# Three columns of a two-row product taken row by row in two chunks of a fused recurrence and feed-forward kernel

## The chip, the cores and the metric

The kernel runs on one core of one Trainium2 chip. A core has TensorE (PE: matrix products, with its weight loads shown apart as PEld), VectorE (DVE), ScalarE (ACT), GpSimd (POOL) and SyncE (SP), each with its own queue of instructions, taken in order. Products land in PSUM, which has eight banks of 128 partitions by 512 float32; everything else sits in SBUF. DMA transfers are issued from the queues of SP, POOL and ACT. The metric is the device time of one execution in microseconds (us), lower is better.

## The reference

A gated linear recurrence over 768 steps, for 4 batch rows and 8 heads of dimension 48, is followed by a bilinear feed-forward layer on the 3072 tokens (4 x 768) of width 8 x 48 = 384, with a hidden width of 1536. All inputs and the output are float32.

```
for t in range(S):
    state = alpha[:, :, t, :, None] * state + einsum('bhd,bhe->bhde', k[:, :, t], v[:, :, t])
    y[:, :, t] = einsum('bhd,bhde->bhe', q[:, :, t], state)
x = y.transpose(0, 2, 1, 3).reshape(B * S, H * D)
out = ((x @ w_a) * (x @ w_b)) @ w_out
```

## The kernel before

The work is cut into six chunks, 0 to 5. A chunk is two batch rows by 256 steps: chunk c takes rows `c % 2 * 2` and the one after it, and the third `c // 2` of the steps. For each chunk the kernel first does the recurrence in its chunked form, with logarithms of alpha, cumulative sums, exponentials, scores and a carried state, and then the feed-forward layer on the chunk's 512 tokens.

The order of all instructions is written out by hand, in the string `PROGRAM` (lines 17 to 258). A line is `chunk: operation; operation; ...`. The program is walked from top to bottom and every operation appends its instructions to the queues of the engines it uses, so the order in `PROGRAM` is the order on each engine; engines run ahead of one another as far as the data, the PSUM banks and the buffers allow. The operations that matter here:

- `XT u` (line 762): the DMA transpose, issued from SP, that brings row u of x from `ys` into `xT`. `X u` before it copies the finished row from PSUM to `ys`. `xT` has a part for each row u = 0, 1. In chunk 2 the program has `XT 1` first and `XT 0` after it; in chunk 3 it has `XT 0` first.
- `a f w i` and `b f w i` (line 777): the gate and the up product of column f (f = 0 to 11, 128 hidden units each) into PSUM bank i. Each is three matmuls, over three slices of the 384 model columns. `w` is `*` for both rows at once (512 tokens wide), `0` or `1` for one row (256 tokens wide, and half of the bank).
- `as f w` (line 783): ScalarE copies the gate product from PSUM to a buffer in SBUF. There are three such buffers, and a half takes a whole one.
- `pr f w` (line 791): VectorE multiplies that buffer with the up product in PSUM, into `prod`.
- `o m h i` (line 799): half h of the output product of token block m; `ot m E` evicts it on engine E (V is VectorE, S is ScalarE), `st m Y` stores it, from SP.
- `lx V` (lines 424 and 427): VectorE adds the logarithms of the even and odd steps of a later chunk, in three instructions. `R 0` and `R 1` (line 488): VectorE takes the remainders after rounding of these sums; `AQ` then uses both.
- `mk u`, `mq u` (line 543): VectorE multiplies keys and queries with their decays; `T u` (line 595), from SP, transposes the result.
- `lv` (line 517) scales keys or queries on VectorE or POOL; `E` are exponentials and `ra` a ratio on ScalarE; `ld` are loads; `dr` and `dl` write the decays to memory and load them again (lines 549 and 554); `K`/`KA`, `k` (lines 653 and 654), `D`, `M`, `Mc`, `Mm`, `SB`, `SA` and `Y` are the recurrence's own state, scores and outputs.

A PSUM bank may be written again only when its last reader is done: for a gate product that is `as`, for an up product it is `pr`, for an output it is `ot`. The bank numbers in `PROGRAM` are chosen by hand.

Chunks 0 and 1 take many of their columns one row at a time. Chunks 2 to 5 take every column with both rows at once. The feed-forward work of chunk 2 begins behind the output products of chunk 1 and is mixed with the preparations of chunks 3 and 4; that of chunk 3 begins behind the output products of chunk 2 and is mixed with those of chunks 4 and 5.

Of the kernel before, what the change touches and what calls it, by code (L numbers as in the profile page):

```python
# [138 lines left out]
1: o 0 1 -; ot 0 V; a 1 1 6; a 10 1 1; as 1 1; as 10 1  # L139
3: E 0 b; E 0 i  # L140
1: b 4 1 2; pr 4 1; b 8 1 5; b 1 1 1; a 8 1 6; b 10 1 0; pr 1 1; o 3 0 2; pr 10 1; as 8 1; pr 8 1; o 3 1 -; ot 3 S; st 3 Y
2: a 4 * 7; as 4 *
3: E 1 b
2: a 5 * 6; b 4 * 3
3: E 1 i
1: st 0 Y
3: dr; ld k * P; lv 0 k P; lv 1 k P
4: lx V; R 0
3: mk 0 V; mq 0 V; T 0
4: ld q * Y  # L150
2: a 1 * 2; b 5 * 0; as 5 *; pr 5 *
4: ra 1
2: b 7 * 4; b 10 * 1; pr 4 *; a 10 * 6; as 10 *; pr 10 *
3: mk 1 V
2: a 7 * 0; b 1 * 5; a 0 * 6; b 0 * 7; as 1 *; as 7 *; pr 1 *; pr 7 *; as 0 *; a 3 * 0; b 9 * 1; pr 0 *
3: mq 1 V; ld v * P
5: ld a * P
2: as 3 *; b 3 * 2; a 9 * 6
4: ra 0
2: pr 3 *; as 9 *; pr 9 *; a 2 * 5  # L160
4: lv 0 q P
2: as 2 *; b 2 * 7; pr 2 *
3: KA * 06; D 0 0 4; M 0 0; dl; k * 0 V; k * 1 V
# [21 lines left out]
2: o 2 0 1; o 2 1 -; o 3 0 6; o 1 0 0; o 3 1 -; o 1 1 -  # L185
4: dr
1: st 1 Y
3: a 11 * 5
2: ot 2 V; ot 3 V
4: mq 0 V; mk 0 V  # L190
5: lx V
3: a 9 * 3; a 0 * 2; a 8 * 6; b 11 * 7; as 9 *; as 11 *; as 0 *; pr 11 *; b 9 * 2; b 0 * 1; pr 9 *
5: lv 0 k V
3: as 8 *
2: ot 1 S
3: b 8 * 3; a 5 * 4; as 5 *; a 6 * 6; a 4 * 7; pr 0 *; pr 8 *
5: R 0
4: mq 1 V
3: b 5 * 3; a 1 * 1; pr 5 *; as 4 *; b 6 * 7; as 6 *; pr 6 *
4: ld v * P; K * 0 2; T 0; D 0 1 5  # L200
3: as 1 *
4: D 0 0 3; Mc 0 0; dl; k * 0 V
# [753 lines left out]
```

## Time and profile before

| what | value |
|---|---|
| median of 3 runs | 196.31 us (195.17 to 201.79) |
| the profiled execution's own time | 196.55 us |
| its span, first to last instruction | 194.8 us |
| instructions | 5851 |
| PE busy | 183.4 us (94%) |
| VectorE busy | 137.2 us (70%) |
| ScalarE busy | 103.0 us (53%) |
| POOL busy | 55.8 us (29%) |
| gate and up products, line 777 | 113.2 us of PE in 540 matmuls |
| output products, line 799 | 48.5 us of PE in 276 matmuls |
| mean granted clock of TensorE | 1.000 |

The profile is of one execution. Its times count from the start of the span. A row of a timeline gives the start, the time from the first start to the last end of the instructions that it merges, the engine, the line, the operation with output and input, the count, and in brackets how long the engine had been idle before it and what it then waited for. Matmuls overlap one another in the array, so their pace is read from start to start, not from the duration of one. The chain is the sequence of work that ended last, followed back from the last instruction.

### The profile page before, as it was taken

What the parts mean: (1) busy time and instruction counts of PE and PEld (TensorE: products, weight loads), DVE (VectorE), ACT (ScalarE), POOL (GpSimd) and SP (SyncE); (2) the same over time, 40 slices, a digit from 0 to 9 for tenths busy, and PEclk for the clock granted to TensorE, in tenths of its full rate; (3) what the DMA queues carried; (4) which work ended last, traced back from release to release, by engine and by line L of the source; (5) the groups of instructions that cost most, each with busy time, mean ns of one, the idle gap of its engine ahead of it and who ended that gap; (6) DMA issues with size and microseconds to landing.
All of it is one profiled execution on the core that took longest, in us unless ns stands there. A gap on an engine that the chain in (4) does not pass through costs nothing.

```text
span 194.8 us, 5851 instructions
## 1 busy us (share of the span) xinstructions
PE 183.4 (94%) x2498; PEld 111.5 (57%) x2498; DVE 137.2 (70%) x230; ACT 103.0 (53%) x189; POOL 55.8 (29%) x75
## 2 busy tenths in 40 slices
PE   1998899899999999999998989999999999999993
PEld 1577675566687877644555534555544556544463
DVE  3588966999899796779979379786755871147520
ACT  4465766686765668555566035766245712154401
POOL 8999734860640424400512400040000000000000
PEclk9999999999999999999999999999999999999999
DMA  5999999999999997999996996566388005013013
GB/s 127 263 214 188 237 231 257 245 247 258 255 228 232 189 252 142 127 267 226 131 237 131 131 277 150 111 51 78 82 156 183 3 3 112 9 43 121 2 40 122
DMA packets 57882, 30.96 MB, mean 159 GB/s; under 512 B 47824, under 2 KB 54880, under 8 KB 57856
## 3 DMA queue, kind: packets, MB, share of 16 engines
q0 software_dynamic: 19680, 18.09, 49.0%
q1 hardware_dynamic: 38032, 12.41, 31.5%
q8 instruction: 19, 0.31, 0.6%
q10 hardware_dynamic: 144, 0.10, 0.2%
q14 instruction: 7, 0.06, 0.1%
HBM read 25.98 MB, written 4.74 MB: 158 GB/s over the span
## 4 chain that ended last, share of the span: by engine, by line
PE 75%; DMA 10%; POOL 8%; issue 2%; DVE 2%; ACT 2%; POOLq 0%; ACTq 0%; DVEq 0%
PE psum L777 43%; PE psum L799 20%; DMA wb_t<-in_moe_w_b_dram 7%; DMA xT<-ys 3%; PE psum L665 3%; PE psum L715 2%; PE psum L618 2%; DVE prod L791 1%; POOL a_t L404 1%; PE psum L498 1%; PE psum L689 1%; PE psum L694 1%; POOL wa_t L384 1%; PE psum L810 1%; POOL v_t L404 1%
## 5 line engine op out<-in xcount | busy, mean ns | idle before, releaser
L777 PE MATMUL psum<-xT,wb_t 128*128 128x512 bf16 (+1 forms) x270 | 57.1, 337 | 0.8 <-DVE prod L791 0.3
L777 PE MATMUL psum<-xT,wa_t 128*128 128x512 bf16 (+1 forms) x270 | 56.1, 337 | 0.7 <-DMA xT<-ys 0.7
L799 PE MATMUL psum<-wo_t,prod 128*128 128x384 bf16 x276 | 48.5, 326 | 0.7 <-issue 0.7
L777 PEld LDWEIGHTS <-wb_t 128*128 128x128 bf16 x270 | 25.6, 98 | 21.6 <-issue 1.1
L777 PEld LDWEIGHTS <-wa_t 128*128 128x128 bf16 x270 | 25.4, 98 | 20.5 <-issue 1.2
L799 PEld LDWEIGHTS <-prod 128*128 128x128 bf16 x276 | 26.2, 98 | 17.6 <-issue 0.7
L517 POOL TENSOR_TENSOR q_t<-q_t,ra 128x384 f32<-128x384 f32 x8 | 9.1, 1135 | 46.8 <-ACT ra L510 32.0
L674 ACT ACTIVATE m<-psum 128x1024 bf16<-128x1024 f32 x16 | 16.2, 1022 | 6.3 <-PE psum L665 6.3
L816 DVE COPY ot<-psum 128x384 f32<-128x384 f32 (+1 forms) x13 | 6.9, 538 | 16.5 <-PE psum L799 14.1
L814 ACT ACTIVATE ot<-psum 128x384 f32<-128x384 f32 (+1 forms) x12 | 5.7, 477 | 12.9 <-PE psum L799 11.9
L678 DVE TENSOR_TENSOR m<-m,mask 128x1024 bf16<-128x1024 bf16 x16 | 11.6, 732 | 0.4 <-ACT m L674 0.4
L543 DVE TENSOR_TENSOR QKp<-k_t,invb 128x768 bf16<-128x768 f32 x10 | 11.1, 1114 | 0.2
L411 ACT ACTIVATE la<-a_t 128x1536 f32<-128x1536 f32 (+2 forms) x9 | 9.5, 1057 | 3.2 <-DMA a_t<-in_alpha_dram 3.1
L670 DVE TENSOR_TENSOR m<-psum,mask 128x1024 bf16<-128x1024 f32 x8 | 9.7, 1218 | 1.6 <-PE psum L665 1.5
L543 DVE TENSOR_TENSOR QKp<-q_t,beta 128x768 bf16<-128x768 f32 x10 | 9.3, 946 | 0.0
L517 POOL TENSOR_TENSOR k_t<-k_t,a_t 128x384 f32<-128x384 f32 x5 | 4.9, 992 | 14.8 <-DMA k_t<-in_k_dram 14.8
L404 POOL DMA_DIRECT2D a_t<-in_alpha_dram x7 | 7.4, 1059 | 5.5 <-DVE prod L791 2.9
L665 PE MATMUL psum<-kqT 64*64 64x128 bf16 x384 | 8.6, 218 | 0.5 <-DVE prod L791 0.2
L453 PE MATMUL psum<-la,ut 128*128 128x192 f32 x16 | 4.7, 448 | 4.2 <-ACT la L411 4.2
L404 POOL DMA_DIRECT2D v_t<-in_v_dram x8 | 8.5, 1066 | 0.1
L665 PEld LDWEIGHTS <-kqT 64*64 64x64 bf16 x384 | 6.4, 107 | 2.9 <-issue 2.5
L755 ACT ACTIVATE ys<-psum 128x768 bf16<-128x768 f32 x7 | 5.6, 809 | 4.3 <-PE psum L694 2.3
(271 smaller groups left out, 274.6 us busy)
## 6 DMA issues: line engine op xcount, KB each, us to landing
out_dram<-ot SPq DMA_DIRECT2D x23, 192.0 KB, 2.6
a_t<-in_alpha_dram POOLq DMA_DIRECT2D x4, 768.0 KB, 11.4
k_t<-in_k_dram POOLq DMA_DIRECT2D x4, 768.0 KB, 8.2
q_t<-in_q_dram POOLq DMA_DIRECT2D x3, 768.0 KB, 10.3
v_t<-in_v_dram POOLq DMA_DIRECT2D x4, 384.0 KB, 6.2
a_t<-in_alpha_dram POOLq DMA_DIRECT2D x3, 384.0 KB, 5.6
q_t<-in_q_dram POOLq DMA_DIRECT2D x3, 384.0 KB, 14.1
k_t<-in_k_dram POOLq DMA_DIRECT2D x3, 384.0 KB, 14.0
```

Of the source, the lines that this page charges most:

```text
L404: eng.dma_start(out=t[:, us, hs].rearrange("p b h r d -> p (b h) (r d)"), in_=src[ch.b0 + us.start:ch.b0 + us.stop, hs, ch.s * 2 * C:(ch.s ...
L411: nc.scalar.activation(out=ch.la[:, us, hs].rearrange("p b h r d -> p (b h r d)"), in_=ch.a[:, us, hs].rearrange("p b h r d -> p (b h r d) ...
L517: eng.tensor_mul(x, x, by)
L543: eng.tensor_mul(QKp[ch.c % 2][:, u, j, :, hs, :D], src[:, u, hs].rearrange("p h r d -> p r h d"), f)
L665: nc.tensor.matmul(s2[g * HC:(g + 1) * HC, r, p, rk, :], lhsT=ch.kqT[u][rs, 1, rk, 2 * h + p, g * HC:(g + 1) * HC], rhs=queriesT(ch, u, 2 ...
L670: nc.vector.tensor_mul(m.rearrange("p r a k s -> p (r a) (k s)"), ch.s2[u, h].rearrange("p r a k s -> p (r a) (k s)"), maskn(4))
L674: nc.scalar.activation(out=m.rearrange("p r a k s -> p (r a) (k s)"), in_=ch.s2[u, h].rearrange("p r a k s -> p (r a) (k s)"), func=AF.Copy)
L678: eng.tensor_mul(x, x, maskn(4))
L777: nc.tensor.matmul(p, lhsT=(wa_t, wb_t)[w][:, kk, f * 128:(f + 1) * 128], rhs=ch.xT[:, us.start // 2:us.stop // 2, kk].rearrange("p u g s ...
L799: nc.tensor.matmul(op, lhsT=ch.prod[:, f, at:at + C], rhs=wo_t[:, f, :], start=(f == 0), stop=(f == NFF - 1))
L814: nc.scalar.activation(out=o_, in_=i_, func=AF.Copy)
L816: eng.tensor_copy(o_, i_)
```

## The change

In chunk 2, columns 4, 5 and 1, and in chunk 3, columns 11, 9 and 0, are computed first for row 0 (`a f 0`, `as f 0`, `b f 0`, `pr f 0`) and then for row 1, in place of both rows in one. With it, bank numbers of these and the following columns are new, the order of the following columns of both stages is somewhat different, `R 0` of chunk 4 moves down behind `mq 1` and a load of chunk 3, and in chunk 3's stage `lx` of chunk 5 comes behind the products of row 0 and `ot 1` of chunk 2 behind `as 5`. What is computed stays the same.

```
-2: a 4 * 7; as 4 *
+2: a 4 0 7; as 4 0; b 4 0 3
 3: E 1 b
-2: a 5 * 6; b 4 * 3
+2: a 5 0 6; as 5 0; b 5 0 0
 3: E 1 i
 1: st 0 Y
 3: dr; ld k * P; lv 0 k P; lv 1 k P
-4: lx V; R 0
+4: lx V
+2: pr 4 0
 3: mk 0 V; mq 0 V; T 0
 4: ld q * Y
-2: a 1 * 2; b 5 * 0; as 5 *; pr 5 *
+2: a 1 0 5; as 1 0; b 1 0 1; a 4 1 2; b 4 1 3; a 5 1 7; a 1 1 4; pr 5 0; as 4 1; pr 1 0; b 5 1 6; b 1 1 5
 4: ra 1
-2: b 7 * 4; b 10 * 1; pr 4 *; a 10 * 6; as 10 *; pr 10 *
+2: a 10 * 2; as 5 1; b 10 * 1; pr 4 1; pr 5 1; a 7 * 7; as 1 1; as 10 *; pr 1 1; pr 10 *; b 7 * 0; as 7 *
 3: mk 1 V
-2: a 7 * 0; b 1 * 5; a 0 * 6; b 0 * 7; as 1 *; as 7 *; pr 1 *; pr 7 *; as 0 *; a 3 * 0; b 9 * 1; pr 0 *
+2: a 0 * 6; pr 7 *; b 0 * 4; as 0 *; a 3 * 3; b 9 * 5; pr 0 *
 3: mq 1 V; ld v * P
+4: R 0
 5: ld a * P
-2: as 3 *; b 3 * 2; a 9 * 6
+2: as 3 *; b 3 * 2; a 9 * 0
 4: ra 0
-2: pr 3 *; as 9 *; pr 9 *; a 2 * 5
+2: pr 3 *; as 9 *; pr 9 *; a 2 * 1
...
-3: a 11 * 5
+3: a 11 0 5; as 11 0
 2: ot 2 V; ot 3 V
 4: mq 0 V; mk 0 V
+3: b 11 0 7; a 9 0 3; as 9 0; b 9 0 2; a 0 0 4; as 0 0; b 0 0 1; pr 11 0; pr 9 0; pr 0 0
 5: lx V
-3: a 9 * 3; a 0 * 2; a 8 * 6; b 11 * 7; as 9 *; as 11 *; as 0 *; pr 11 *; b 9 * 2; b 0 * 1; pr 9 *
+3: a 11 1 6; as 11 1; b 11 1 7; a 9 1 5; as 9 1; b 9 1 2; a 0 1 3; as 0 1; b 0 1 4; pr 11 1; pr 9 1; pr 0 1
 5: lv 0 k V
-3: as 8 *
+3: a 8 * 6; as 8 *; b 8 * 1; a 5 * 2; as 5 *; a 6 * 3; a 4 * 5; pr 8 *
 2: ot 1 S
-3: b 8 * 3; a 5 * 4; as 5 *; a 6 * 6; a 4 * 7; pr 0 *; pr 8 *
 5: R 0
 4: mq 1 V
-3: b 5 * 3; a 1 * 1; pr 5 *; as 4 *; b 6 * 7; as 6 *; pr 6 *
+3: b 5 * 4; a 1 * 1; pr 5 *; as 4 *; b 6 * 7; as 6 *; pr 6 *
```

## The prediction

> **What bounds the kernel now.** I read the page first: the busy shares, the chain and the costliest groups.
>
> ```profile
> span 194.8 us, 5851 instructions
> PE 183.4 (94%) x2498; PEld 111.5 (57%) x2498; DVE 137.2 (70%) x230; ACT 103.0 (53%) x189; POOL 55.8 (29%) x75
> PE 75%; DMA 10%; POOL 8%; issue 2%; DVE 2%; ACT 2%; POOLq 0%; ACTq 0%; DVEq 0%
> L777 PE MATMUL psum<-xT,wa_t 128*128 128x512 bf16 (+1 forms) x270 | 56.1, 337 | 0.7 <-DMA xT<-ys 0.7
> ```
>
> The first line is the span of the one profiled execution, whose whole time was 196.55 us, 1.75 more. The median of the three runs is 196.31, so both may be used within 0.24. TensorE (PE) is busy 94% of the span and carries 75% of the chain. The gate products (L777) waited 0.7 us in all, and what ended that wait is a transfer: the DMA transpose that brings x into `xT`. An average does not say what the two edited stages are worth, so next I read the windows of these two stages and of what comes after them (columns: length, then busy us of PE, PEld, DVE, ACT, POOL, the granted clock, DMA).
>
> ```profile
> 81.74:93.40 11.66, 11.66 (x56) 5.17 (x53) 10.06 (x15) 6.97 (x14) 0.00 (x0) 1.00 1.17 230
> 112.10:122.10 10.00, 9.32 (x44) 4.04 (x42) 8.48 (x13) 4.41 (x9) 0.00 (x0) 1.00 0.85 205
> 128.00:132.00 4.00, 3.57 (x137) 2.34 (x126) 2.83 (x6) 2.62 (x4) 0.71 (x1) 1.00 1.04 84
> 136.00:188.00 52.00, 52.00 (x476) 27.16 (x474) 27.17 (x42) 19.95 (x33) 0.00 (x0) 1.00 0.29 67
> ```
>
> Chunk 2's gate and up work (81.74 to 93.40) has PE busy 11.66 of 11.66 us: no gap to fill. Chunk 3's (112.10 to 122.10) has 9.32 of 10.00: 0.68 idle. From 136 to 188 PE is never idle, so time won on PE before that reaches the end unless something turns late. The gap in chunk 3 is seen in PE's timeline and in the chain, in order of time:
>
> ```profile
> 106.27 6.01 PE L799 MATMUL psum<-wo_t,prod 128*128 128x384 bf16 x36 [0.69 <-issue]
> 112.96 2.75 PE L777 MATMUL psum<-xT,wa_t 128*128 128x512 bf16 x12 [0.68 <-DMA xT<-ys]
> 115.55 2.75 PE L777 MATMUL psum<-xT,wb_t 128*128 128x512 bf16 x12
> 106.61 6.22 DMA xT<-ys
> 103.44 1.99 SPq L762 DMA_TRANSPOSE xT<-ys  x1
> 106.61 2.15 SPq L762 DMA_TRANSPOSE xT<-ys  x1
> ```
>
> The 36 output products of chunk 2 end at 112.28; the first gate column of chunk 3 starts at 112.96. It reads both rows of `xT`, and the later one (row 1, issued at 106.61 in program order `XT 0`, then `XT 1`) lands 6.22 us after its issue, at 112.83. Row 0's transpose was issued at 103.44, 3.17 us earlier; with the same 6.22 it is there by 109.66, before PE is free.
>
> **The change, part by part.**
>
> *PE work.* In each chunk, three columns with gate and up are six groups of three 512-wide matmuls. They become twelve groups of three 256-wide ones, with 18 matmuls and 18 weight loads more per chunk, 36 of each in all. The 256-wide form is in the trace, in chunk 1:
>
> ```profile
> 62.62 1.47 PE L777 MATMUL psum<-xT,wa_t 128*128 128x256 bf16 x12
> 63.93 0.82 PE L777 MATMUL psum<-xT,wb_t 128*128 128x256 bf16 x6
> 62.51 1.30 PEld L777 LDWEIGHTS <-wa_t 128*128 128x128 bf16 x12
> ```
>
> From start to start, twelve 256-wide matmuls take 63.93 - 62.62 = 1.31 us, 0.109 each; twelve 512-wide ones take 115.55 - 112.96 = 2.59, 0.216 each. Two halves cost 2 x 0.109 - 0.216 = about 0.0025 us more than a whole, so 36 x 0.0025 = 0.09 us. The loads run beside the matmuls: twelve in 1.30 us, the same pace. If that cover went, each of the 36 new loads would cost at most its own 1.30 / 12 = 0.108, 3.9 us.
>
> [...]
>
> *Chunk 3: the wait.* `a 11 0` needs row 0 alone. PE's next start after 36 output products at (6.01 - 0.33) / 35 = 0.162 (0.33 being the duration of the last) is 106.27 + 36 x 0.162 = 112.11 in place of 112.96: 0.85 us won. The six groups of row 0 take 36 / 2 x 0.109 = 1.96 us and last until 114.07; row 1 has landed at 112.83, 1.2 us before it is wanted. Bounds of this gain: 0 (row 0 lands late too, or row 1's landing was a chance of this execution) and 0.85. I take 0.85, as every row says it.
>
> *Chunk 2: the same edit without a wait.* There the program issues `XT 1` first and `XT 0` last, so row 0 is the later one. PE is busy to 81.74 with chunk 1's output and finds both landed. The edit gains nothing here.
>
> *ScalarE and VectorE.* Six copies (`as`) and six products (`pr`) of 512 become twelve of each.
>
> ```profile
> 78.06 0.38 ACT L783 ACTIVATE as__1713<-psum 128x256 bf16<-128x256 f32 x1 [0.65 <-PE psum L777]
> 78.38 0.38 ACT L783 ACTIVATE as__1715<-psum 128x256 bf16<-128x256 f32 x1
> 114.45 0.60 ACT L783 ACTIVATE as__2305<-psum 128x512 bf16<-128x512 f32 x1 [7.44 <-PE psum L777]
> 114.95 0.59 ACT L783 ACTIVATE as__2307<-psum 128x512 bf16<-128x512 f32 x1
> 80.06 0.45 DVE L791 TENSOR_TENSOR prod<-as__1715,psum 128x256 bf16<-128x256 bf16 x1 [0.21 <-ACT as__1745 L783]
> 80.40 0.43 DVE L791 TENSOR_TENSOR prod<-as__1745,psum 128x256 bf16<-128x256 bf16 x1
> 116.47 0.73 DVE L791 TENSOR_TENSOR prod<-as__2307,psum 128x512 bf16<-128x512 bf16 x1 [1.23 <-PE psum L777]
> 117.09 0.71 DVE L791 TENSOR_TENSOR prod<-as__2305,psum 128x512 bf16<-128x512 bf16 x1
> ```
>
> Start to start a copy is 0.32 (256) against 0.50 (512), so a pair costs 0.14 more; a product 0.34 against 0.62, 0.06 more. Per chunk that is 3 x 0.14 = 0.42 us of ScalarE and 3 x 0.06 = 0.18 of VectorE. Before its first copy ScalarE sat idle 7.44 us, VectorE 1.23 before its first product: both cover it. Cost 0; uncovered, at most 0.42 per chunk.
>
> *The order on VectorE, chunk 3.* It is in-order, and here the edit is delicate: the three half products of row 0 go ahead of chunk 5's crossed pairs (`lx`), the three of row 1 behind them, and each frees a PSUM bank that a later column takes.
>
> ```profile
> 111.82 0.95 DVE L543 TENSOR_TENSOR QKp<-q_t,beta 128x768 bf16<-128x768 f32 x1
> 112.69 0.95 DVE L543 TENSOR_TENSOR QKp<-k_t,invb 128x768 bf16<-128x768 f32 x1
> 113.55 0.55 DVE L424 TENSOR_TENSOR l<-la 128x384 f32<-128x384 f32 x1
> 114.11 1.12 DVE L427 TENSOR_TENSOR l<-la 64x384 f32<-64x384 f32 x2
> ```
>
> `mq 0` and `mk 0` stay first. `pr 11 0` starts at 113.55, `pr 9 0` at 113.89; `pr 0 0` waits for `b 0 0` (PE until 114.07, plus the tail of a matmul, 0.17) and starts near 114.3. `lx` then runs from 114.65 to 116.33 (113.55 to 115.23 before, 1.68). The row 1 products start at 116.33, 116.67 and 117.01. On PE, row 1's six groups run from 114.07 to 116.03, `a 8` and `b 8` (0.65 each) to 117.33, and `a 5` then wants bank 2, which `pr 9 1` frees at 116.67 + 0.45 = 117.12. Margin 0.2 us: no stall. `b 11 1` wants bank 7 at 114.40, free at 114.0. The `as` buffers are three, and a half takes a whole one; the fourth copy waits for the first product, done at 114.0, and is wanted at 114.6. `R 0` and `mq 1` of the later chunks start near 118.4 and 119.3 (119.38 and 120.24 before), so the transpose `T 1` behind `mq 1` on SP is not later. `ot 1` moves behind two copies on ScalarE by about 1 us; its store comes far later in SP's queue.
>
> *The order on VectorE, chunk 2.* `R 0` of chunk 4 (0.95) leaves the place ahead of `mk 0` and `pr 4 0` (0.45) comes in.
>
> ```profile
> 82.45 0.96 DVE L488 TENSOR_TENSOR lh<-l 128x768 f32<-128x768 f32 x1
> 83.33 0.95 DVE L543 TENSOR_TENSOR QKp<-k_t,invb 128x768 bf16<-128x768 f32 x1
> 85.21 2.95 SPq L595 DMA_TRANSPOSE kqT<-QKp  x1
> 91.07 0.94 DVE L543 TENSOR_TENSOR QKp<-q_t,beta 128x768 bf16<-128x768 f32 x1
> ```
>
> `pr 4 0` adds a wait: it needs `b 4 0`, which PE ends at 81.74 + 6 x 0.109 + 0.17 = 82.56. Behind it on VectorE are `mk 0` and `mq 0`, and behind these SP's transpose `T 0` (85.21), the row and decay loads and chunk 4's q load. `mk 0` would start near 82.95 against 83.33, so all are earlier by some 0.4. `mq 1` comes near 90.4 against 91.07. `b 4 1` wants bank 3 at 84.0, free at 83.05. `R 0` goes behind `mq 1`; its reader is `R 1`, ten us later. Nothing here reaches PE, which is full. The edits of this part cost 0; uncovered, a late VectorE would cost PE the lateness itself, below 1 us.
>
> **Sum.** -0.85 + 0.09 = -0.76 us. On the profiled execution 196.55 - 0.76 = 195.8; on the median 196.31 - 0.76 = 195.55, which I give as 195.6. What is late next: in the region of 128 to 132 PE has 0.43 us of gaps behind VectorE, which itself waits for PE and so moves along. Of the transfers that do not move, chunk 4's decay load is nearest:
>
> ```profile
> bl<-row SPq DMA_DIRECT2D x8, 3.0 KB, 5.5
> 116.77 1.08 SPq L554 DMA_DIRECT2D bl<-row  x2
> 123.50 0.56 DVE L654 TENSOR_TENSOR Sm<-tmp,bl 128x384 bf16<-128x384 f32 x1
> ```
>
> Its second issue, near 117.3, lands near 122.8 by the median; its reader would want it at 122.7 in place of 123.50, level, with no wait to speak of.
>
> **Rivals.**
>
> 1. *No gain.* Row 0's matmuls still wait for row 1 (the change doesn't do what it says), or the 6.22 us were a chance of this execution, since the median from issue to landing is half of it. Then 196.31 + 0.09 = 196.4. Against the first: half-width matmuls start while the other half of `xT` is still to be written, in chunk 0.
>
> ```profile
> xT<-ys SPq DMA_TRANSPOSE x8, 3.1
> ...
> L777 PE MATMUL psum<-xT,wa_t x270: 269/379/390, 18.6 to 183.0; 128*128 128x512 bf16 x81, 128*128 128x256 bf16 x54
> L757 DVE CAST xT<-psum x1: 957/957/957, 24.9 to 24.9; 128x768 bf16<-128x768 f32 x1
> ```
>
> 18.6 is before 24.9, the only copy of that kind, which writes row 1.
>
> 2. *Slower: VectorE holds a bank.* `lx` (1.68 us) sits between the two sets of products in chunk 3. Once it starts more than 0.2 us later than worked out, `a 5` waits for bank 2, and PE loses the excess. The worst that the rows give is a whole `lx` and a product, 1.68 + 0.45 - 0.2 = 1.9 us: 195.6 + 1.9 = 197.5. For it: VectorE is busy 8.48 of these 10 us. Against it: it had 1.23 us of slack there.
>
> 3. *Slower: the loads set the pace.* With weight loads partly bare, the 36 new ones cost between 0 and 3.9 us (the row of twelve loads); half of them bare is 2 us: 195.6 + 2 = 197.6. Against it: the 0.109 us pace of the 256-wide matmuls, with their loads in it. [...]
>
> 4. *A larger gain.* All of PE's gaps from 104 to 132 closed: 0.69 + 0.85 + 0.43, about 2 us: 194.4. No row shows why the 0.69 (its cause is "issue") should go.
>
> **How the numbers follow.** Chances: forecast 0.50 (195.2 to 196.0), no gain 0.22 (to 196.9), bank held 0.14, loads 0.06, larger gain 0.04, something beyond all these 0.04. From 194.4 to 197.9 the range takes in all but the worst of rivals 2 and 3. A change of 2%, 3.9 us, is about what a measurement of this kernel can tell from none. Faster by that would need twice all of PE's gaps here: 0.02. Slower by that needs every new load bare, or a stall that no row shows: 0.06. Within: 0.92.
>
> **What would show it.** The first gate matmul of chunk 3 without the wait on `xT`, starting close behind the output products; 256-wide groups at 0.109 us; the windows of chunk 2 as full as before; `a 5` of chunk 3 with no wait on a product; PE full to the end. The forecast is wrong if row 0's landing is late as well, if `a 5`, `b 4 1` or `mk 0` wait, or if the 256-wide pace is above 0.12.

## The result and the profile after

In the ratio to the kernel before, the changed kernel was 0.6% slower: 1.0059, 95% interval 1.0033 to 1.0085, where the forecast had 0.9961 (195.55 / 196.31). The median of 20 executions is 197.44 us (195.67 to 205.57), inside the range given and 1.8 above the forecast. The ratio leaves out executions well above the fastest of their kernel, 12 of before's 20 (201.39 to 205.52 us) and 4 of after's, the profiled one among them, so that the median over all of before's (202.09) lies above 197.44 although the ratio is above 1, and whatever a late transfer did in those executions does not count in it.

The profiled execution of after took 199.62 us, 3.07 more than that of before and 2.2 above its own median, so it shows more of the loss than a usual one has. What a usual execution of after loses is not seen in a trace. Lines of the new kernel stand two higher (L777 is now L779, L799 is L801). First the page:

```profile
span 197.8 us, 5952 instructions
PE 183.1 (93%) x2534; PEld 115.1 (58%) x2534; DVE 139.3 (70%) x236; ACT 104.4 (53%) x195; POOL 56.8 (29%) x75
PE 69%; DMA 12%; DVE 7%; POOL 6%; issue 3%; ACT 1%; POOLq 0%; DVEq 0%; ACTq 0%
L779 PE MATMUL psum<-xT,wa_t 128*128 128x256 bf16 (+1 forms) x288 | 57.7, 326 | 4.3 <-DMA xT<-ys 3.6
```

PE is busy as long as before (183.1 against 183.4) with 36 matmuls more; the span grew by 3.0 and all of it is waiting. The gate products waited 3.6 us for `xT` in place of 0.7. PE's timeline shows the two places:

```profile
84.50 0.49 PE L779 MATMUL psum<-xT,wa_t 128*128 128x256 bf16 x3 [2.12 <-DMA xT<-ys]
108.47 6.02 PE L801 MATMUL psum<-wo_t,prod 128*128 128x384 bf16 x36
114.33 0.49 PE L779 MATMUL psum<-xT,wa_t 128*128 128x256 bf16 x3
115.96 0.49 PE L779 MATMUL psum<-xT,wb_t 128*128 128x256 bf16 x3
117.92 0.50 PE L779 MATMUL psum<-xT,wa_t 128*128 128x256 bf16 x3 [1.47 <-DMA xT<-ys]
126.24 0.82 PE L779 MATMUL psum<-xT,wb_t 128*128 128x512 bf16 x3
```

Chunk 2's first gate column waited 2.12 us (it had not waited before). Chunk 3's row 0 started without a wait, right behind the output products, but its row 1 waited 1.47. The same places, side by side:

| place on PE | before | after | after behind by |
|---|---|---|---|
| first gate column of chunk 2 | 81.74 | 84.50 | 2.76 |
| 36 output products of chunk 2 | 106.27 | 108.47 | 2.20 |
| first gate column of chunk 3 | 112.96 | 114.33 | 1.37 |
| first up column behind chunk 4's `K` | 123.19 | 126.24 | 3.05 |
| end of the span | 194.8 | 197.8 | 3.0 |

What lies ahead of the first row is the same program in both, so 2.76 of the 3.0 is nothing that the new order did. Of the rest, 0.56 us was won as the gap of 0.69 in front of the output products was gone, 0.83 because row 0 did not wait (forecast 0.85), and 1.68 was lost again, 1.47 of it on row 1. From the first gate column of chunk 2 on, the sum is +0.24 in place of -0.76.

The windows of the stages that the prediction showed, at their new places:

```profile
84.50:96.30 11.80, 11.79 (x74) 6.94 (x73) 9.69 (x16) 7.16 (x17) 0.00 (x0) 1.00 0.96 206
114.33:126.24 11.91, 10.44 (x125) 6.68 (x123) 10.03 (x18) 5.56 (x12) 0.00 (x0) 1.00 0.83 180
140.00:190.00 50.00, 50.00 (x464) 25.95 (x462) 26.72 (x40) 19.41 (x31) 0.00 (x0) 1.00 0.29 67
```

Chunk 2's stage is full, chunk 3's has lost 1.47, and from 140 on PE is never idle. The chain, in order of time, has both transposes:

```profile
77.91 6.55 DMA xT<-ys
110.03 7.85 DMA xT<-ys
```

Issued at 110.03, row 1 of chunk 3 landed 7.85 us later, at 117.88. What else was on its way is seen in POOL's timeline, first of before, then of after:

```profile
105.92 0.99 POOL L517 TENSOR_TENSOR k_t<-k_t,a_t 128x384 f32<-128x384 f32 x1 [7.79 <-DMA k_t<-in_k_dram]
106.86 1.19 POOL L404 DMA_DIRECT2D v_t<-in_v_dram  x1
108.04 1.15 POOL L404 DMA_DIRECT2D q_t<-in_q_dram  x1
```

```profile
106.89 1.36 POOL L519 TENSOR_TENSOR k_t<-k_t,a_t 128x384 f32<-128x384 f32 x1 [7.11 <-DMA k_t<-in_k_dram]
108.20 1.19 POOL L406 DMA_DIRECT2D v_t<-in_v_dram  x1
109.39 1.16 POOL L406 DMA_DIRECT2D q_t<-in_q_dram  x1
```

Before, the transpose (issue 106.61) stood 0.25 us ahead of chunk 4's v load. After, it (110.03) stood 1.83 behind that load and 0.64 behind the q load. POOL is not held by chunk 3's work on PE: its load goes when its own product of keys is done, and that waits for a DMA. VectorE's timeline tells why the transpose was late, before and after:

```profile
104.50 1.01 DVE L517 TENSOR_TENSOR k_t<-k_t,a_t 128x384 f32<-128x384 f32 x2
105.62 0.96 DVE L757 CAST ys<-psum 128x768 bf16<-128x768 f32 x1
```

```profile
107.30 1.84 DVE L519 TENSOR_TENSOR k_t<-k_t,a_t 128x384 f32<-128x384 f32 x2
109.06 0.94 DVE L759 CAST ys<-psum 128x768 bf16<-128x768 f32 x1
```

The two key products ahead of `X 1` took 1.84 us in place of 1.01, while POOL's own key product (106.89 to 108.25) ran beside them, and `X 1`, which `XT 1` needs, came behind them. PE itself was late as well. Its inner products of chunk 3's row 1, which `X 1` evicts, before and after:

```profile
105.01 0.57 PE L715 MATMUL psum<-v_t,m 64*128 64x48 bf16 x32
```

```profile
107.81 0.72 PE L717 MATMUL psum<-v_t,m 64*128 64x48 bf16 x32
```

They start 2.80 us later than before, while POOL's v load is only 1.34 later. PE was behind by 2.76 already at chunk 2's first gate column. So in this execution most of the lateness of `XT 1` (3.42) comes from ahead of the edit.

### The profile page after: what moved, and what is told of

It reads as the page before. It is cut to its first block, busy times and chain, and to the rows that moved or that the text cites. A ratio compares the mean times of both kernels' runs of the same rounds, so it can differ in the third digit from the quotient of the medians.

```text
span 197.8 us, 5952 instructions
## 1 busy us (share of the span) xinstructions
PE 183.1 (93%) x2534; PEld 115.1 (58%) x2534; DVE 139.3 (70%) x236; ACT 104.4 (53%) x195; POOL 56.8 (29%) x75
## 4 chain that ended last, share of the span: by engine, by line
PE 69%; DMA 12%; DVE 7%; POOL 6%; issue 3%; ACT 1%; POOLq 0%; DVEq 0%; ACTq 0%
PE psum L779 41%; PE psum L801 17%; DMA xT<-ys 7%; DMA wb_t<-in_moe_w_b_dram 4%; PE psum L667 2%; DVE m L680 2%; DVE prod L793 2%; PE psum L620 2%; PE psum L691 2%; PE psum L717 1%; PE psum L812 1%; ACT m L676 1%; POOL v_t L406 1%; POOL a_t L406 1%; DVE k_t L519 1%
## 5 line engine op out<-in xcount | busy, mean ns | idle before, releaser
L779 PE MATMUL psum<-xT,wa_t 128*128 128x256 bf16 (+1 forms) x288 | 57.7, 326 | 4.3 <-DMA xT<-ys 3.6
L779 PE MATMUL psum<-xT,wb_t 128*128 128x256 bf16 (+1 forms) x288 | 58.8, 326 | 0.9 <-DMA wb_t<-in_moe_w_b_dram 0.6
L801 PE MATMUL psum<-wo_t,prod 128*128 128x384 bf16 x276 | 48.5, 326 | 0.0
L779 PEld LDWEIGHTS <-wa_t 128*128 128x128 bf16 x288 | 27.3, 98 | 22.6 <-issue 2.8
L779 PEld LDWEIGHTS <-wb_t 128*128 128x128 bf16 x288 | 27.4, 98 | 19.7 <-DMA wb_t<-in_moe_w_b_dram 0.8
L801 PEld LDWEIGHTS <-prod 128*128 128x128 bf16 x276 | 26.1, 98 | 17.0
L680 DVE TENSOR_TENSOR m<-m,mask 128x1024 bf16<-128x1024 bf16 x16 | 12.4, 785 | 0.4 <-ACT m L676 0.4
L519 POOL TENSOR_TENSOR k_t<-k_t,a_t 128x384 f32<-128x384 f32 x5 | 5.8, 1170 | 13.1 <-DMA k_t<-in_k_dram 13.1
```

Source lines behind the costliest of these rows:

```text
L519: eng.tensor_mul(x, x, by)
L680: eng.tensor_mul(x, x, maskn(4))
L779: nc.tensor.matmul(p, lhsT=(wa_t, wb_t)[w][:, kk, f * 128:(f + 1) * 128], rhs=ch.xT[:, us.start // 2:us.stop // 2, kk].rearrange("p u g s ...
L801: nc.tensor.matmul(op, lhsT=ch.prod[:, f, at:at + C], rhs=wo_t[:, f, :], start=(f == 0), stop=(f == NFF - 1))
```

## The experiments

**Theory.** The landing of chunk 3's row 1 is no fixed 6.22 us. It is a race between `XT 1` on SP and POOL's loads of v and q. The edit helps to lose it: chunk 2's 36 matmul and load instructions shift the place of PE's gap marked "issue" (0.69 us in before, ahead of its output products), and that delays `X 1`. (The profile of after has no such gap of over 0.25 us; other kernels below have it.) **Rivals.** The order of VectorE or the banks of the new stages; the pace of narrow matmuls; the edit of one chunk alone.

### One half of the edit at a time

`c2_only` has the new lines of chunk 2 alone, `c3_only` those of chunk 3 alone:

```
c2_only   2: a 4 0 7; as 4 0; b 4 0 3 ...     3: a 11 * 5 ...
c3_only   2: a 4 * 7; as 4 * ...              3: a 11 0 5; as 11 0 ...
```

> Chunk 2's part of the change alone; chunk 3 as before. Theory A (loads ahead of the transpose): the chunk 2 part moves the loads on POOL earlier against PE, so that they are issued ahead of chunk 3's second x transpose and hold its landing; the first gate matmul of chunk 3, which here wants both rows, then waits 1.5 to 2.5 us (0.68 before), ratio 1.004 to 1.010. Theory B (the halves themselves cost, on PE, ScalarE or VectorE): half of the loss, ratio 1.003, with no longer wait on xT. Theory C (the landings differ by chance from execution to execution, and the order has no part in it): ratio 1.000 within the interval.

> Chunk 3's part alone; chunk 2 as before. Theory A: the loads stand where they stood, row 0 starts without the wait and row 1 has landed in time: 0.85 us won, ratio 0.995 to 0.998. Theory B: the other half of the loss, ratio 1.003. Theory C: ratio 0.996 to 1.000.

Measured: `c2_only` 199.90 us (198.47 to 201.23), ratio 1.0199 [1.0136, 1.0262]; `c3_only` 200.63 (197.19 to 204.03), ratio 1.0116 [1.0040, 1.0192]. Each half alone reads slower than both. PE's timeline of `c2_only`, and of `c3_only`:

```profile
105.91 0.40 PE L717 MATMUL psum<-v_t,m 64*128 64x48 bf16 x18 [0.94 <-issue]
114.85 2.75 PE L779 MATMUL psum<-xT,wa_t 128*128 128x512 bf16 x12 [2.58 <-DMA xT<-ys]
```

```profile
106.65 6.01 PE L799 MATMUL psum<-wo_t,prod 128*128 128x384 bf16 x36 [0.48 <-issue]
117.02 0.50 PE L777 MATMUL psum<-xT,wa_t 128*128 128x256 bf16 x3 [2.40 <-DMA xT<-ys]
```

In `c2_only` the gap that before has in front of its output products has moved: 14 of the 32 inner products of chunk 3's row 1 are out (the row holds the other 18), then PE stands for 0.94 us. `X 1` comes after them, at 106.35, and `XT 1` at 107.33, behind v (106.24). The chain of `c2_only`:

```profile
107.33 7.38 DMA xT<-ys
```

The 18 that are left are 18 weight loads and 18 matmuls, 36 instructions, as many as the edit adds in chunk 2. In `c3_only` the gap is where before has it. There VectorE's key products were slow, as in after; v went at 106.45 and `XT 1` at 107.81. VectorE and the chain of `c3_only`:

```profile
105.09 1.83 DVE L517 TENSOR_TENSOR k_t<-k_t,a_t 128x384 f32<-128x384 f32 x2
106.84 0.94 DVE L757 CAST ys<-psum 128x768 bf16<-128x768 f32 x1
```

```profile
107.81 9.16 DMA xT<-ys
```

So the race is lost in two ways here, and the second needs nothing of the edit: up to `XT 1`, `c3_only` is the program of before. The landing after the issue that the prediction took as given is 6.22, 7.38, 7.85 or 9.16 us.

### Holding the loads until the transposes have landed

`gate_after` and `gate_before`: POOL copies one element of the landed `xT` ahead of the loads of v and a (chunk 2) and of v and q (chunk 3), so that these cannot go first.

```
+ nc.gpsimd.tensor_copy(go, <xT, row 0 of chunk 2>)     ahead of the loads of v, a
+ nc.gpsimd.tensor_copy(go, <xT, row 1 of chunk 3>)     ahead of the loads of v, q
```

> The changed kernel, with two copies of one element on POOL that read xT, row 0 of chunk 2 and row 1 of chunk 3, ahead of the loads of v and alpha and of v and q: these loads are issued only when the second x transpose of the chunk has landed. Theory A: the transposes land about 3 us after their issue, no wait on xT in chunk 2 nor chunk 3, ratio to the kernel before 0.990 to 0.997, unless the loads, some 2 us later, are then late for their readers. Theory B: ratio 1.006 as without the gates.

> The kernel before with the same two gates on POOL. Theory A: the second transposes land about 3 us after their issue, the wait of 0.68 us ahead of chunk 3 is gone, ratio 0.994 to 0.998. Theory B and C: ratio 1.000; if the loads become late for their readers, over 1.000.

Measured: 198.94 us (197.66 to 200.34), ratio 1.0146 [1.0084, 1.0207], and 200.68 (198.41 to 201.6), ratio 1.0195 [1.0116, 1.0273]. Neither ratio came as expected. The gate columns no longer wait for `xT`: with these loads held back POOL's copy, which waits for the landing, starts 3.71 and 4.02 us after the issue of the transpose in chunk 2 (80.07 - 76.36 and 81.30 - 77.28) and some 2.9 and 4.6 after it in chunk 3 (at 112.04 and 113.41; an estimate, with the issue 0.98 behind the start of `X 1`, as in `c2_only`). But the loads come back later. PE and the chain of `gate_after`:

```profile
100.06 0.18 PE L699 MATMUL psum<-Sm,kqT 64*64 64x48 bf16 x1 [2.02 <-DVE prod L796]
107.70 0.40 PE L720 MATMUL psum<-v_t,m 64*128 64x48 bf16 x18 [1.29 <-issue]
125.09 0.64 PE L670 MATMUL psum<-kqT 64*64 64x128 bf16 x32 [1.30 <-DMA kqT<-QKp]
```

```profile
92.77 4.74 DMA bl<-row
115.44 9.60 DMA kqT<-QKp
```

The v and q loads, now at 112.61 and later, meet the next transpose, of keys and queries, which takes 9.60 us. So it is the loads that make transposes late, and holding them for too long only moves the wait. The second row shows the gap inside the inner products once more, in a kernel that has chunk 2's edit.

### Moving PE's gap without the edit, and back with it

Counted over matmuls and weight loads in the trace, in the order of their starts, 3261 stand ahead of PE's gap in before, `c2_only`, `c3_only` and both gated kernels (and later in `ygate_before` and `ygate_after`), whatever the next instruction does. The page's row of instruction transfers fits this, before and after:

```profile
q8 instruction: 19, 0.31, 0.6%
```

```profile
q8 instruction: 20, 0.33, 0.7%
```

If these 19 packets of 0.31 MB / 19 = 16 KB are PE's, they bring 2 x 2498 matmuls and loads, 263 to a packet, and the 20 of after bring 2 x 2534, 253 to a packet (estimates). If a gap belongs to a packet's first instruction, 36 instructions more ahead of it move it, and a packet's count more puts the next one in its place; 256, between the two estimates, was taken for it. `pad18_before` has 18 tiny pairs of load and matmul (36 instructions, as many as chunk 2's edit) ahead of chunk 2's first gate column. The `pad110` kernels have 110 pairs at the start of PE, so that the edit's 36 and these 220 make 256 (`pz`, in all four, writes the pairs' zeros on VectorE):

```
pad18_before                             0: pz; c1a; ...   2: pad 18 7; a 4 * 7; as 4 *
pad110_before, pad110_after, pad110_c2   0: pz; pad 110 2; c1a; ...
```

> The kernel before, every column of both rows at once, with 18 idle pairs of weight load and tiny matmul (2 columns of zeros) on PE ahead of chunk 2's first gate column: as many PE instructions, 36, as the chunk 2 part adds, and nothing else. Theory D (PE's instruction stream is fetched in blocks; a stall stands at a fixed count of instructions, and 36 more move it from behind chunk 3's row 1 inner products into them, which delays that row's eviction and its x transpose past the loads on POOL): the stall of about 1 us is found inside the inner products (line 715's), the second x transpose of chunk 3 is issued after the load of v, the first gate matmul of chunk 3 waits 2 to 3 us, ratio 1.010 to 1.020, nearly all that chunk 2's part alone cost. Theory B (the halves themselves cost): only the pairs' own time, 0.5 to 1 us, ratio 1.003 to 1.005, and the stall or the wait unchanged.

> The kernel before with 110 such pairs at PE's very start, where it waits for alpha: 220 instructions, which move the stall to 18 pairs behind its place, into chunk 2's output products. Control for the pairs themselves. Theory D: no loss by the stall, ratio 0.998 to 1.004, unless the pairs make PE late at the start. Theory B: the same.

> The changed kernel with the 110 pairs at PE's start: 220 and chunk 2's 36 make 256, so chunk 3's stall stands where it stood in the kernel before. Theory D: the inner products of row 1 run through, the second transpose is issued about where it was, and row 0's groups hide its landing: no wait ahead of chunk 3, ratio to before 0.993 to 1.000 and below the changed kernel's 1.006. Theory B: 1.006 or more.

> Chunk 2's part alone with the 110 pairs at PE's start. Theory D: the stall is back behind the inner products, the wait ahead of chunk 3 falls from 2.6 us to below 1, ratio 0.998 to 1.005 against 1.020 without the pairs. Theory B: 1.015 or more.

| kernel | median (lowest to highest) | ratio [interval] |
|---|---|---|
| pad18_before | 202.24 (197.95 to 207.86) | 1.0111 [1.0040, 1.0182] |
| pad110_before | 204.47 (194.46 to 206.24) | none |
| pad110_after | 197.93 (195.85 to 208.21) | 1.0017 [0.9969, 1.0065] |
| pad110_c2 | 196.93 (194.55 to 205.58) | 0.9990 [0.9943, 1.0037] |

Thirty-six instructions without any of the edit cost the kernel before 1.1% by a ratio that rests on two executions (197.95 and 199.17 us), and with 256 in all `c2_only` goes from 1.0199 to 0.9990, its intervals apart. After goes from 1.0059 to 1.0017, with intervals that overlap. `pad110_before`, the control, took over 202 us in four of five executions and so says nothing of the pairs' own cost. PE's timeline of `pad110_after` has the gap back at the output products, longer than in before, with 3516 matmuls and loads ahead of it (255 more than 3261), and no wait for `xT`:

```profile
106.80 7.68 PE L807 MATMUL psum<-wo_t,prod 128*128 128x384 bf16 x36 [1.69 <-issue]
```

`pad18_before` is less clean: no gap of over 0.25 us was seen near the inner products in its profile, and VectorE's key products were slow (104.87, 1.83 us), so there the race was lost in the second way. PE's timeline shows what that costs with both rows at once:

```profile
116.00 5.28 PE L783 MATMUL psum<-xT,wa_t 128*128 128x512 bf16 x12 [3.89 <-DMA xT<-ys]
```

It waits 3.89 us, and the twelve matmuls then take 5.28 in place of 2.75. `pad110_before` has the same at 119.95 (4.46 and 5.28), with `XT 1` 1.83 us behind v. So has `pad110_c2` in its one profile, an execution of 205.58 us, where a wait below 1 us was expected:

```profile
119.09 5.28 PE L785 MATMUL psum<-xT,wa_t 128*128 128x512 bf16 x12 [3.88 <-DMA xT<-ys]
```

There VectorE's key products took 1.84 us and `XT 1` (110.72) was 1.83 behind v (108.89). So the ratios agree with the theory that the gap's place decides the race, and the gap does move by the count of instructions; that its place is what made `pad110_c2` faster was not seen in a trace.

### Putting the transpose ahead of the loads

`order_before` moves chunk 4's key products on VectorE behind `X 1` and `XT 1`. `ygate_before` adds a copy on POOL of one element of `ys`, row 1, ahead of the loads: they wait until `X 1` has written it, no longer. `ygate_after` and `ygate_c3` are after and `c3_only` with both.

```
-4: ld k * P; lv 1 k V; lv 0 k V
+4: ld k * P
... (behind 3: X 1 V; XT 1)
+4: lv 1 k V; lv 0 k V
...
+3: gy 1                    (ygate only: POOL reads one element of ys, row 1)
 4: ld v * P; ...
```

> The kernel before with chunk 4's two k products on VectorE (lv 1 k, lv 0 k) moved behind chunk 3's eviction of row 1 (X 1), so that this eviction no longer waits for them when they run beside POOL's k product and take 1.8 us in place of 1.0. Theory E (a race: if chunk 3's second x transpose is issued after the load of v on POOL, it lands 7.4 to 9.2 us after its issue, and PE waits; if before, 3 to 6 us): the transpose is issued at 0.1 us after the inner products' end plus one eviction of 0.96 in every execution, ahead of the load of v more often, the wait ahead of chunk 3 below 1 us, ratio 0.996 to 1.002 and fewer executions above 201 us. Theory D alone (the instruction stall): no difference.

> The same, and a copy of one element on POOL that reads chunk 3's ys of row 1 ahead of the load of chunk 4's v: the loads of v and q are issued only when the eviction is done, which is when the second transpose is issued. Theory E: the transpose is never behind the loads; wait ahead of chunk 3 between 0 and 1 us, hardly any execution above 199 us, ratio of the medians of all runs well below 1, of the others 0.996 to 1.002.

> The changed kernel with both of these. Theory E: row 0 starts without a wait and row 1 has landed when it is wanted; the stall of PE's instruction stream inside the inner products delays the transpose by some 0.8 us, but the loads wait for it. Ratio to the kernel before 0.993 to 1.000, against 1.006 without. Theory B (the halves cost): 1.004 or more.

> Chunk 3's part alone with both of these. Theory E: the 0.85 us that row 0 was to win appears here, with no stall inside the inner products: ratio 0.992 to 0.998, against 1.012 for the part alone. Theory B: 1.002 or more.

Measured, without ratios: 199.08 us (198.13 to 200.62), 195.54 (194.97 to 198.22), 196.28 (195.31 to 196.93), 195.87 (194.58 to 197.55); before beside them had a median of 201.19 (197.4 to 205.49). The order on VectorE alone did not do it: in `order_before` v (106.59) was still ahead of `XT 1` (107.82), which took 7.33 us, and PE waited 2.54. That is a third way to lose the race: there was no gap and no slow key product, but PE had waited 0.97 us for `xT` at chunk 2's first gate column, and `X 1` waited for PE. With the loads held by `ys` nothing waits for `xT` in chunk 3 in these three profiles. POOL and PE of `ygate_before`:

```profile
105.71 0.44 POOL L856 CAST go<-ys 1x1 f32<-1x1 bf16 x1 [0.83 <-DVE ys L759]
106.10 1.19 POOL L406 DMA_DIRECT2D v_t<-in_v_dram  x1
```

```profile
105.53 6.01 PE L801 MATMUL psum<-wo_t,prod 128*128 128x384 bf16 x36 [0.89 <-issue]
111.38 2.75 PE L779 MATMUL psum<-xT,wa_t 128*128 128x512 bf16 x12
```

Here both rows at once wait for nothing: 111.38 is right behind the output products. The wait that the edit was to remove is then not there.

### What the edit costs with the race held

The ygate kernels again, unchanged, with more executions (`held_before`, `held_after`; then, on another chip, `held_before2`), with each half of the edit (`held_c2`, `held_c3`), and with 110 pairs at the start (`held_pad_after`).

```
held_before = held_before2 = ygate_before;  held_after = ygate_after;  held_c3 = ygate_c3
held_c2 = c2_only with both moves;  held_pad_after = held_after with 0: pz; pad 110 2; ...
```

> The kernel before with chunk 4's key products on VectorE moved behind `X 1` and `XT 1` of chunk 3, and POOL's loads of chunk 4's v and q held until row 1 of chunk 3's `ys` is written (as in ygate_before), timed in more rounds. If loads issued ahead of the second transpose of chunk 3 are what costs the kernel before (they add a late landing, a wait of some 4 us and half pace behind it), this kernel is faster than before by more than 2%: median 195 to 196.5 beside some 200. If they matter only where the edit puts them there, it is as before, within 0.5%.

> The changed kernel with the same two things. If the order of transpose and loads is the whole of the edit's cost, this kernel is level with held_before, or ahead of it by up to the 0.76 us of the prediction's sum. If the stall of TensorE inside the inner products of chunk 3's row 1 (moved there by the 36 new instructions of chunk 2) costs something by itself, or the new order in the two stages does, it is slower than held_before by 0.3 to 1 us.

> The kernel held_before once more, as the foot that the other three runs of this set are compared with. Expected: a median of 195.5 to 196.2, within 0.5% of its first one, 195.84.

> held_before with the edits of chunk 2 alone, which bring no wait away and move TensorE's stall into the inner products of chunk 3's row 1. If that stall's place (or chunk 2's new order) is the 0.56 us by which held_after was slower than held_before, this kernel is slower than held_before by 0.4 to 0.8 us, as held_after was. If the edits of chunk 3 are the cause, it is level with held_before.

> held_before with the edits of chunk 3 alone, which leave TensorE's stall behind these inner products. If the stall's place or chunk 2's order costs the 0.56 us, this kernel is level with held_before or up to 0.7 us faster, since row 0 can start ahead of row 1's landing. If chunk 3's own order costs it, it is slower by 0.4 to 0.8 us.

> held_after with 110 tiny weight loads and matmuls ahead of everything on TensorE, which with the 36 of the edit make 256 instructions, so that the stall is back behind the inner products of chunk 3's row 1. If the stall's place is the 0.56 us, this kernel is level with held_before or faster by up to 0.7 us; the added pairs can cost some 0.1 us at the start. If chunk 2's or chunk 3's order is the cause, it stays slower than held_before by 0.4 to 0.8 us.

| kernel | median (lowest to highest), executions | ratio to before [interval] |
|---|---|---|
| held_before | 195.84 (194.88 to 199.88), 12 | 0.9973 [0.9937, 1.0009] |
| held_after | 196.40 (195.92 to 198.29), 12 | 1.0021 [0.9980, 1.0062] |
| held_before2 | 195.53 (195.31 to 195.98), 5 | 0.9963 [0.9929, 0.9998] |
| held_c2 | 196.13 (195.18 to 196.53), 5 | 0.9978 [0.9937, 1.0019] |
| held_c3 | 195.74 (195.26 to 196.22), 5 | 0.9967 [0.9930, 1.0004] |
| held_pad_after | 198.70 (196.24 to 201.30), 5 | 1.0069 [0.9991, 1.0146] |

The 2% that was expected of `held_before` did not come in the ratio (0.3%) and came nearly in the median over all (195.84 beside 198.82, 1.5%).

The single executions say more than the ratio. Over 200 us took 52 of the 95 executions of before in all these comparisons, 3 of the 20 of after and 3 of the 6 of `c3_only`; none did of the 22 of `ygate_before`, `held_before` and `held_before2`, nor of the 32 of the edited kernels with the loads held and no pairs added. In the profiles in which both rows at once waited 3.88 us or more for `xT`, the execution took 202.24 to 206.24; where row 0 went first and row 1 was late, the wait was 1.47 (after) or 2.40 (`c3_only`), in executions of 199.62 and 198.72. This points to the lost race as what takes before over 200 us, and to the row-by-row order as what makes it cheaper. It is not shown: no execution of before over 200 us was profiled.

With the race held the whole edit still costs 0.56 us by the medians; chunk 2's half reads 0.60 slower (196.13 - 195.53) and chunk 3's 0.21, both less than the scatter of `held_c2` (195.18 to 196.53) over five executions. What remains leans to chunk 2, which had no wait to lose, but the held kernels leave chunk 2's own race open: in `held_c2`'s profile the v load (77.12) went ahead of `XT 0` (77.35), and PE waited 1.11 us there. Whether the place of the gap carries it is open: `held_after`'s profile has it inside the inner products,

```profile
106.15 0.40 PE L719 MATMUL psum<-v_t,m 64*128 64x48 bf16 x18 [1.26 <-issue]
```

but `held_pad_after`, which was to put it back and win the 0.56, was slower by 2.3 us (198.70 beside 196.40). Its gap was there, 2.50 us long, behind 3517 matmuls and loads, just 256 more than 3261, with slow output products behind it (7.69 us for 36):

```profile
110.09 7.69 PE L809 MATMUL psum<-wo_t,prod 128*128 128x384 bf16 x36 [2.50 <-issue]
```

The test therefore settles nothing. The profiles of the first pair (spans of 194.6 and 194.2) do not show the 0.56 either: `held_before`'s had still a wait on row 1, 0.96 us, with the transpose 0.43 ahead of v and a landing of 6.21. Being ahead of the loads by so little is no sure cure; `held_before2`'s profile, 0.4 ahead as well, had no wait.

`held_before` reads as the fastest kernel of the study, 0.3 to 0.4% below before in the ratio, but the first of its two intervals takes in 1, and `held_c3` is level with it.

## Why the prediction was wrong

- *"`a 11 0` needs row 0 alone", 0.85 us won.* Right: 114.33 is right behind the output products, and the place gained 0.83.
- *"Row 1 has landed at 112.83, 1.2 us before it is wanted."* **The step that failed.** It took one execution's landing (6.22 us from an issue at 106.61) for a property of the program. In after it landed 7.85 us after an issue that itself came 0.66 us later against chunk 2's start, and row 1 waited 1.47: more than the 0.85 won. The halves did not make that landing late by themselves. With both rows at once PE would have started at the same 117.92 with row 0's six groups (1.96 us) still to do, an estimate from the prediction's pace. What failed is the taking of the landing as given. The rows for it were there: v's load at 106.86 was 0.25 us behind the transpose, on another queue, and nothing held that order. Rival 1 named the chance but gave it the price of no gain (196.4), not of a loss.
- *"36 x 0.0025 = 0.09 us."* Right as a pace, incomplete as a cost. Four groups behind one another start at 84.50, 84.83, 85.16 and 85.48, 0.327 for three, 0.109 each; chunk 2's stage from `a 4` to the inner products took 11.80 us against 11.75. No run shows the 2.3 us in the top of the range (195.6 + 2.3 = 197.9); the runs showed these 0.109 us a matmul, its load beside it, and 0.05 us on the stage. What was not costed is that instructions also shift the place of a gap (0.69, "issue") that the prediction listed only as a gain that no row explains. `pad18_before`, 36 instructions and no edit, read 1.1% slower, on two executions and with no gap in its profile.
- *"The edit gains nothing here", chunk 2.* Right that nothing was to be won, perhaps too kind: with the race held this half alone read 0.60 us slower, within its scatter. The wait of 2.12 in after's profile comes from a landing issued behind POOL's v load (77.91 against 77.41), on queues that the edit leaves as they were up to there, and shows as well in `ygate_c3` (1.81) and, with `XT 0` only 0.04 us ahead of the load, in `order_before` (0.97), which have no edit in chunk 2. So that `XT 0` landed in time in the prediction's trace, 0.38 us ahead of that load (77.43 against 77.81), was one outcome of a race too.
- *VectorE and banks.* Right. VectorE's timeline of after:

```profile
116.98 0.55 DVE L426 TENSOR_TENSOR l<-la 128x384 f32<-128x384 f32 x1
117.54 1.12 DVE L429 TENSOR_TENSOR l<-la 64x384 f32<-64x384 f32 x2
118.88 0.45 DVE L793 TENSOR_TENSOR prod<-as__2348,psum 128x256 bf16<-128x256 bf16 x1 [0.21 <-ACT as__2348 L785]
```

`lx` runs between the two sets of products, ends at 118.66 and holds nothing: the next product waits for ScalarE, and from 117.92 to 126.24 PE has no wait for a bank of these columns. With row 1 late, `lx` had more room there than the 0.2 us of the prediction; in `ygate_after` and `held_after`, where row 1 was not late, no wait of over 0.25 us was seen there either. Rival 2 and rival 3 did not happen, though their times (197.5 and 197.6) are near the measured one; that the range held it is luck.
- *A gain with a sure landing?* With the race held, chunk 3's half was level with `held_before` (+0.21), since both rows at once then mostly wait for nothing. Starting row 0 early is worth something only in executions in which row 1 is late, and there at most the 1.96 us of row 0's groups. Taking row 1 first in chunk 2, the order in which its transposes are issued, was not tried.

So the cause is settled in part. Shown: the landing is late when the loads of the other queue go first; PE's gap moves with the count of instructions; with the loads held until `X 1` is written, chunk 3 waits over 0.25 us for `xT` in one of nine profiles (`held_before`, 0.96 us). Argued: that the shift of the gap is how the edit loses the race in usual executions; it is seen in `c2_only`, not in after. Open: what the last 0.56 us are, and whether the lost race is what takes before over 200 us.

## What to carry to other kernels

A landing time read from one execution is a value of that race, not of the program (6.21 to 9.16 us for row 1 of chunk 3 here): before a gain is booked on it, look at which other queues issue near it (here from 1.84 us ahead to 0.43 behind) and what holds their order. Instructions that cost next to nothing in pace (0.05 us on chunk 2's stage) can still shift a gap, which here stood behind the same 3261 of them, and if one marked "issue" lies near a critical transfer, ask where it will lie after the edit. A load may be held behind the write that the urgent transfer needs, but not for longer: held until the landing, it met the next transfer (9.60 us).

## What the hardware showed beside

- PE's gaps marked "issue" in the stretch between chunks 2 and 3 were 0.40 to 2.50 us, one each in 13 of the 20 profiles. In six profiles whose chunk 2 had waited 0.97 us or more for `xT` (after, `held_c2`, `ygate_c3`, `order_before`, `pad110_before`, `pad110_c2`) no such gap of over 0.25 us came there, and none in `pad18_before`, which had no such wait. That PE waits there for a packet of instructions was not shown. It agrees with the 253 to 263 matmuls and loads to a packet of 16 KB (estimates) and with the gap's shift by 255 and 256 (`pad110_after`, `held_pad_after`). Most packets would then cost no gap that shows: with 19 in before and 20 in after, a profile has one such gap at most in this stretch, and in the six whose waits on PE are known over the whole span (before, after, `c2_only`, `c3_only`, `gate_after`, `gate_before`) none of over 0.25 us comes elsewhere; `pad110_before` has one of 0.37 us at 28.21. The one that shows can still be 2.50 us (`held_pad_after`).
- A transpose of `xT` issued behind loads of POOL's queue landed 7.33 to 9.16 us after its issue in chunk 3 and 5.54 to 6.55 in chunk 2; with the loads held until it had landed, POOL's copy behind it started some 2.9 to 4.6 us after the issue (`gate_after`, `gate_before`). Issued 0.25 and 0.43 us ahead of the loads it took 6.22 and 6.21 in chunk 3.
- Behind PE waits of 3.88 to 4.46 us the matmuls ran at half pace (5.28 against 2.75 us for twelve), and the granted clock was 0.84 over 101 to 121 us in `pad18_before`, where `ygate_before` had 1.00. Half pace for a part of the matmuls came after gaps of 1.69 (`pad110_after`, 36 output products in 7.68 against 6.01) and 2.50 and after the wait of 2.54 in `order_before` (4.44 for twelve) too, but not after 2.58 in `c2_only` (2.75 for twelve; granted clock 1.00 over the execution). The length of the wait alone does not decide it.
- VectorE's two key products took 1.83 us in place of 1.01 in five profiles in which POOL's key product began 0.12 to 0.41 us before or after them.
